# Block-sparse attention and Fourier mixing: clears ahead of the warm-up's copy, two q copies on ScalarE, fills in place of table operations, and a remade order

## Chip, cores, metric

One core of a Trainium2 chip. The metric is the device time of one execution in microseconds, here the median of three runs. A profile is one execution taken by the hardware profiler; its span runs from the first to the last instruction. Engines: TensorE (PE), VectorE (DVE), ScalarE (ACT), GpSimd (POOL), and SyncE (SP), which here only issues transfers.

## What is computed

Inputs q, k, v of shape (4, 8, 768, 64); each query block of 64 attends to its own key block and to the three blocks with the highest gate scores, causally. The result goes through a Fourier mixing layer and a two-layer perceptron with 512, 2048 and 512 features.

```python
k_rep = k.reshape(B, H, 12, 64, D).mean(axis=3)
gate = where(causal, einsum('bhsd,bhnd->bhsn', q, k_rep), -1e9)
sel = top 3 blocks of gate, and the own block
scores = where(sel & causal, scale * q @ k.T, -1e9)
x = softmax(scores) @ v                     # to (B, S, 512)
u = x + real(fft(fft(x, axis=1), axis=2))
un = (u - mean(u)) / sqrt(var(u) + 1e-6)
out = u + relu(un @ w_ch1) @ w_ch2
```

## The kernel before

Two heads make a pair P (0 to 15, four to a batch b). All work is cut into small steps with two-letter names, and the string `ORDER` (line 112) lists them; a loop at line 755 records them in that order. Each engine executes its own instructions in the order in which they stand in the list; between engines only semaphores order them. So a step can be listed late and still run early, if its engine's queue has nothing open ahead of it, and it can be held by a step that it has nothing to do with, if that one stands ahead of it on the same engine.

The steps of attention, with line and engine: loads `Lk`, `Lq`, `Lv` (L270, L275, SP queue); `tk`, `tq`, transposes of k and q on PE into PSUM (L292); `ks`, block sums of k on DVE (L297); `kh`, their spread to two heads (L222, DVE); `kc`, k to SBUF on ACT (L308, L311); `qc`, q to SBUF in f32 (L316, DVE); `qs`, q to f16 on POOL (L225); `g`, gate scores on PE (L335, L342); `gt`, their transpose and bounds on DVE (L349 to L358); `gx`, the eight largest of each row (L366); `gl:P,0`, the comparison with the third largest, and `gl:P,1`, the own block cleared (both L222, DVE); `gm`, transpose back, tile mt (L386); `s:P,i`, six score tiles (L409, L414), with mask products of mt and indz for P below 7 (L421); `e:P,i`, the exponential on ACT (L431); `d:P,i`, the triangle on POOL (L437); `vc`, v to f16 on POOL; `v`, attention times v on PE (L449); `x`, the division by the row sum on DVE.

The steps of mixing, for batch b: `fs`, `fd`, `f` folds on DVE; `pg`, a POOL instruction that waits for the folds, ahead of the weights' loads `W` and `X` (POOL queue); `y` on PE (L519, L525), `tr` on DVE (L538) and `ty` on ACT (L532); `m` on PE (L552, L553), `u` on DVE (L566), `xu` on ACT (L578), then the transposes: `xt` on PE and `un` on DVE in batch 0, DMA transposes on SP's queue (L593) in batches 1 to 3; `bn` statistics on DVE. The perceptron: `w` (L629, L631) and `r` (ReLU), then `c` in two halves (L656), `o` on DVE (L668) and `od`, the output's transfer.

PSUM is a pool of four tiles of two banks. If two engines read one such tile, the program makes the one that stands later in the list wait for the other: `ks` and `kc` of a pair, and `tr` and `ty` of one tile.

Before the list runs `consts_first` (L678 on): the first loads of k and q, half each on SP's and ACT's queues; a dummy exponential on ACT; nine warm-up matmuls on zeros, whose result DVE copies (L694); then on DVE a cast of the identity and six clears; and on ACT's queue the loads of three small tables: indc (block indicators, from which `iz:1` and `iz:0` make indz on ACT, L712), lim and oth. The table oth2 is loaded in `consts_next` on SP's queue.

Of the kernel before, what the change touches and what calls it, by code (L numbers as in the profile page):

```python
# [21 lines left out]
NB = 12  # L22
# [6 lines left out]
def _consts_np():  # L29
# [22 lines left out]
    oth = np.where(np.arange(9)[:, None] + 3 != nn, NEG, 0.0)[None].repeat(128, 0)  # L52

    lim = np.where(nn[None, 4:8] > np.arange(3, 7)[:, None], -3e38, 3e38)
    lim = lim.reshape(1, 16).repeat(128, 0).astype(np.float32)

    indc = np.zeros((4, 32, 2, NB), np.float32)
    for g in range(4):
        for n in range(NB):
            indc[g, n, g % 2, n] = 1.0  # L60

    own = 2 * np.arange(5)[None, :] + 2 + (p // 64)[:, None]
    oth2 = np.zeros((128, 5, 2, 16), np.float32)
# [49 lines left out]
Lk:1 Lq:1 Lk:2 Lq:2 tk:0 ks:0 tq:0 Lq:3 Lk:3 kh:0 qc:0 iz:1 tk:1 qs:0 kc:0 g:0 ks:1 iz:0 gt:0 tq:1  # L113
kc:1 gx:0 Lq:4 Lv:0 Lk:4 Lv:1 kh:1 gl:0,0 tk:2 gl:0,1 gm:0 kc:2 qc:1 s:0,3 s:0,2 ks:2 e:0,3 qs:1
tq:2 Lq:5 Lk:5 s:0,5 qc:2 g:1 e:0,5 e:0,2 kh:2 s:0,4 gt:1 qs:2 s:0,0 e:0,4 gx:1 s:0,1 d:0,2 tq:3
gl:1,0 e:0,0 gl:1,1 tk:3 gm:1 e:0,1 d:0,0 qc:3 g:2 d:0,3 kc:3 d:0,5 s:1,5 gt:2 d:0,4 s:1,0 e:1,5
qs:3 ks:3 s:1,4 e:1,0 tq:4 d:0,1 gx:2 vc:0 e:1,4 s:1,3 qc:4 s:1,1 Lv:2 e:1,3 s:1,2 gl:2,0 kh:3
tk:4 gl:2,1 e:1,2 d:1,3 gm:2 g:3 d:1,4 ks:4 d:1,0 v:0 d:1,5 gt:3 vc:1 kc:4 gx:3 e:1,1 s:2,5 Lv:3
Lq:6 LF:0 Lq:7 Lk:6 Lk:7 LT:0 s:2,3 kh:4 gl:3,0 e:2,5 gl:3,1 s:2,4 e:2,3 d:1,1 x:0 tq:5 qs:4 e:2,4
g:4 d:2,3 gm:3 qc:5 s:2,0 d:2,4 s:2,2 d:1,2 e:2,0 gt:4 d:2,5 tk:5 vc:2 gx:4 e:2,2 s:2,1 ks:5 d:2,0  # L120
Lv:4 Lq:8 Lk:8 s:3,1 e:2,1 v:1 gl:4,0 kh:5 gl:4,1 kc:5 d:2,1 gm:4 d:2,2 s:3,2 x:1 e:3,1 vc:3 g:5
e:3,2 Lv:5 Lc:0 d:3,1 s:3,5 gt:5 s:3,0 fs:0,1 e:3,5 s:3,3 d:3,2 gx:5 e:3,0 s:3,4 fs:1,1 tq:6
gl:5,0 e:3,3 fs:0,0 v:2 gl:5,1 fs:1,0 e:3,4 d:3,3 qc:6 d:3,0 s:4,5 x:2 d:3,4 s:4,4 e:4,5 d:3,5
s:4,0 qs:5 v:3 e:4,0 gm:5 fs:2,0 fs:2,1 e:4,4 s:5,5 x:3 s:4,1 e:5,5 s:5,1 e:4,1 fd:2,0 s:4,2 s:5,0
fs:3,1 e:5,1 fs:3,0 s:5,2 fd:2,1 e:5,0 fd:3,1 s:4,3 fd:3,0 e:5,2 tk:6 f:0,1 f:0,2 e:4,3 Lk:9 Lq:9
tk:7 f:0,3 e:4,2 f:0,0 y:0,1 ks:7 pg:0 W:0 kc:6 y:0,0 tr:0,1 d:4,0 kc:7 d:4,4 d:4,5 ks:6 d:5,5
d:4,1 ty:0,1 tr:0,0 s:5,3 d:5,2 s:5,4 d:4,3 kh:6 W:1 ty:0,0 m:0,2 qs:6 e:5,3 u:0,2 m:0,1 vc:4
e:5,4 m:0,0 u:0,1 xu:0,2 d:5,4 tk:8 d:5,1 d:4,2 u:0,0 xu:0,1 d:5,0 xt:0,2 W:2 g:6 un:0,2 xu:0,0
xt:0,1 gt:6 tq:8 un:0,1 kc:8 xt:0,0 qc:8 tq:7 un:0,0 qs:8 v:4 Lq:10 Lk:10 Lv:6 Lq:11 qc:7 bn:0,3
w:0,4 d:5,3 qs:7 bn:0,1 w:0,5 r:0,4 gx:6 ks:8 w:0,6 r:0,5 gl:6,0 kh:7 gl:6,1 x:4 w:0,7 r:0,6 gm:6  # L130
w:0,3 r:0,7 s:6,5 r:0,3 s:6,1 e:6,5 s:6,3 e:6,1 kh:8 s:6,2 fs:4,0 bn:0,4 w:0,2 e:6,2 d:6,1 X:0
e:6,3 g:7 w:0,0 d:6,5 gt:7 r:0,2 d:6,3 vc:6 gx:7 s:6,4 r:0,0 vc:5 s:6,0 e:6,4 tk:9 Li:0 gl:7,0
Lv:7 tq:9 gl:7,1 e:6,0 gm:7 w:0,11 Lq:12 Lv:8 K:7 qc:9 kc:9 g:8 r:0,11 v:5 gt:8 d:6,0 ks:9 w:0,8
qs:9 gx:8 w:0,10 x:5 r:0,8 d:6,4 d:6,2 gl:8,0 s:7,5 s:7,2 r:0,10 kh:9 fs:4,1 w:0,1 bn:0,5 e:7,5
vc:7 e:7,2 tq:10 gl:8,1 Lv:9 r:0,1 X:1 gm:8 s:7,4 qc:10 w:0,15 d:7,2 e:7,4 K:8 bn:0,0 g:9 r:0,15
s:7,0 w:0,9 gt:9 e:7,0 gx:9 vc:8 tq:11 r:0,9 d:7,0 Lv:10 s:7,1 qc:11 d:7,5 tk:10 d:7,4 e:7,1
gl:9,0 s:7,3 ks:10 v:6 e:7,3 kh:10 gl:9,1 kc:10 gm:9 d:7,3 s:8,4 bn:0,2 d:7,1 w:0,12 vc:9 x:6
e:8,4 K:9 Lv:11 Lk:11 Lq:13 Lq:14 Lk:12 Lk:13 v:7 r:0,12 g:10 x:7 s:8,3 w:0,13 e:8,3 gt:10 nv:0
s:9,4 r:0,13 fs:5,1 s:9,1 fs:7,0 vc:11 w:0,14 e:9,4 fs:6,1 e:9,1 fs:7,1 s:8,1 fs:6,0 fs:5,0
c:0,2,0 r:0,14 fd:7,1 fd:6,1 e:8,1 gx:10 s:9,0 fd:7,0 s:9,2 e:9,0 fd:6,0 s:8,2 gl:10,0 c:0,3,0  # L140
f:1,3 e:9,2 f:1,2 e:8,2 gl:10,1 f:1,0 s:8,0 gm:10 s:9,3 d:8,2 e:8,0 y:1,1 d:8,1 d:9,0 e:9,3 nr:0
c:0,0,0 tr:1,1 ty:1,1 s:9,5 c:0,2,1 e:9,5 d:8,0 d:9,3 tk:11 K:10 s:8,5 c:0,1,0 Lk:14 ks:11 kc:11
c:0,3,1 f:1,1 d:9,5 e:8,5 d:9,1 qs:10 tq:12 o:0,2 y:1,0 od:0,2 kh:11 d:8,4 o:0,3 pg:1 vc:10 qc:12
c:0,1,1 od:0,3 ty:1,0 d:9,4 Lv:12 Lv:13 qs:11 tr:1,0 g:11 c:0,0,1 gt:11 d:8,3 d:8,5 gx:11 qs:12
m:1,0 o:0,0 m:1,1 od:0,0 o:0,1 d:9,2 od:0,1 v:8 u:1,1 m:1,2 u:1,0 xu:1,1 c:0,4,0 gl:11,0 xu:1,0
un:1,1 x:8 s:10,3 gl:11,1 un:1,0 c:0,4,1 u:1,2 e:10,3 d:10,3 fs:8,0 s:10,5 s:10,2 bn:1,3 e:10,5
tk:12 e:10,2 fs:8,1 v:9 gm:11 Lk:15 Lq:15 ks:12 xu:1,2 K:11 bn:1,0 tq:13 kc:12 un:1,2 c:0,5,0
qc:13 vc:13 bn:1,4 s:11,2 d:10,5 x:9 s:11,4 vc:12 e:11,2 c:0,5,1 bn:1,1 Lv:14 Lv:15 e:11,4 s:11,0
o:0,5 s:11,5 w:1,11 e:11,5 od:0,5 o:0,4 e:11,0 kh:12 bn:1,5 od:0,4 s:11,3 w:1,7 e:11,3 r:1,11
s:10,1 d:11,3 r:1,7 d:11,0 s:10,0 e:10,1 d:11,4 g:12 d:10,2 tk:13 d:11,5 e:10,0 gt:12 d:11,2  # L150
s:11,1 ks:13 d:10,1 w:1,0 e:11,1 d:10,0 kh:13 fs:9,0 fs:9,1 s:10,4 r:1,0 d:11,1 gx:12 w:1,14
e:10,4 gl:12,0 gl:12,1 g:13 gm:12 r:1,14 d:10,4 w:1,12 K:12 gt:13 kc:13 gx:13 w:1,6 bn:1,2 r:1,12
tq:14 gl:13,0 r:1,6 qs:13 v:10 qc:14 gl:13,1 s:12,3 gm:13 s:12,5 v:11 x:10 e:12,3 K:13 e:12,5
s:12,0 x:11 w:1,8 e:12,0 fs:10,0 vc:15 s:12,1 r:1,8 s:12,2 fs:10,1 s:13,4 e:12,1 d:12,3 w:1,5
fs:11,1 d:12,5 e:13,4 fs:11,0 d:12,1 fd:10,0 w:1,10 r:1,5 fd:11,0 fd:10,1 s:13,0 fd:11,1 r:1,10
w:1,4 f:2,0 e:13,0 f:2,2 s:13,1 f:2,1 e:12,2 w:1,2 e:13,1 tk:14 r:1,4 w:1,3 ks:14 r:1,2 f:2,3
kc:14 s:12,4 kh:14 r:1,3 pg:2 y:2,0 d:13,4 vc:14 nv:1 e:12,4 qs:14 w:1,9 tr:2,0 w:1,13 ty:2,0
d:12,0 r:1,9 g:14 r:1,13 y:2,1 gt:14 gx:14 s:13,2 w:1,1 e:13,2 gl:14,0 gl:14,1 gm:14 s:13,5 w:1,15
tr:2,1 e:13,5 r:1,1 d:13,5 d:13,0 tk:15 ty:2,1 r:1,15 d:12,4 d:12,2 c:1,0,0 kc:15 nr:1 m:2,0 m:2,1
u:2,0 c:1,1,0 d:13,1 K:14 u:2,1 tq:15 ks:15 xu:2,1 s:13,3 bn:2,3 c:1,0,1 xu:2,0 un:2,1 qc:15  # L160
e:13,3 c:1,1,1 un:2,0 d:13,3 d:13,2 s:14,5 v:12 o:1,0 kh:15 od:1,0 o:1,1 v:13 e:14,5 bn:2,1 od:1,1
d:14,5 x:12 qs:15 s:14,3 m:2,2 e:14,3 bn:2,0 c:1,4,0 x:13 fs:13,0 g:15 fs:13,1 c:1,5,0 u:2,2
fs:12,0 xu:2,2 gt:15 c:1,2,0 bn:2,4 un:2,2 gx:15 c:1,5,1 gl:15,0 fs:12,1 gl:15,1 gm:15 bn:2,5
c:1,4,1 K:15 c:1,2,1 o:1,4 od:1,4 o:1,5 s:14,1 od:1,5 s:15,4 e:14,1 s:15,0 c:1,3,0 e:15,4 d:14,1
d:14,3 e:15,0 d:15,4 s:14,4 s:14,2 d:15,0 e:14,4 s:15,2 c:1,3,1 e:15,2 e:14,2 s:15,3 o:1,3 w:2,1
od:1,3 o:1,2 bn:2,2 w:2,2 od:1,2 r:2,1 s:15,5 w:2,4 e:15,5 w:2,15 r:2,4 r:2,2 w:2,3 r:2,15 e:15,3
s:15,1 r:2,3 d:15,3 w:2,9 d:14,4 e:15,1 d:14,2 d:15,2 d:15,5 s:14,0 r:2,9 d:15,1 w:2,14 e:14,0
v:15 d:14,0 w:2,5 x:15 w:2,7 r:2,5 fs:15,1 fs:15,0 r:2,14 fd:15,1 v:14 fd:15,0 r:2,7 w:2,6 x:14
w:2,11 fs:14,0 fs:14,1 fd:14,1 w:2,13 fd:14,0 f:3,2 f:3,0 w:2,10 r:2,13 r:2,11 w:2,8 f:3,3 r:2,10
f:3,1 nv:2 w:2,0 r:2,8 nr:2 r:2,6 y:3,1 r:2,0 y:3,0 ty:3,1 c:2,0,0 pg:3 tr:3,0 tr:3,1 w:2,12  # L170
c:2,1,0 r:2,12 ty:3,0 c:2,0,1 c:2,1,1 m:3,0 o:2,0 c:2,2,0 od:2,0 u:3,0 o:2,1 xu:3,0 m:3,1 od:2,1
c:2,4,0 u:3,1 un:3,0 xu:3,1 bn:3,2 m:3,2 c:2,3,0 u:3,2 un:3,1 bn:3,3 xu:3,2 c:2,5,0 bn:3,0 un:3,2
bn:3,5 c:2,3,1 bn:3,1 c:2,4,1 c:2,2,1 w:3,3 c:2,5,1 r:3,3 o:2,3 w:3,7 od:2,3 o:2,4 o:2,2 od:2,4
w:3,11 r:3,7 od:2,2 o:2,5 w:3,4 r:3,11 od:2,5 w:3,2 bn:3,4 nv:3 w:3,0 r:3,2 nr:3 w:3,8 r:3,0 w:3,1
r:3,8 w:3,13 r:3,1 r:3,4 w:3,6 w:3,10 w:3,9 r:3,10 r:3,13 w:3,5 r:3,6 w:3,14 r:3,5 w:3,12 c:3,2,0
r:3,12 r:3,9 r:3,14 c:3,0,0 w:3,15 c:3,4,0 r:3,15 c:3,1,0 c:3,0,1 c:3,1,1 c:3,5,0 o:3,0 od:3,0
o:3,1 c:3,3,0 od:3,1 o:3,5 od:3,5 c:3,4,1 c:3,2,1 o:3,4 od:3,4 c:3,3,1 c:3,5,1 o:3,3 od:3,3 o:3,2
# [610 lines left out]
```

## Time and profile before

| | |
|---|---|
| runs | 297.56, 297.54 and 297.93 us, median 297.56 |
| profiled execution, span | 295.6 us |
| PE busy | 286.5 us, 97% |
| DVE busy | 192.5 us, 65% |
| ACT busy | 164.2 us, 56% |
| POOL busy | 111.1 us, 38% |
| moved by DMA | 33.53 MB, mean 113 GB/s |
| granted TensorE clock | 1.00 |

Busy shares are means over stages with different limits. In a row of instruction groups stand the line, the engine, the operation, the tiles written and read with their shapes, the count, the busy us, the mean ns of one, and the idle time before it with what ended it. In a timeline row stand start, duration, engine (ACTq, SPq: the transfer queues of ACT and SP), line and operation. Two numbers joined by a dash or "from ... to" are start and end in the timeline, in us from the span's start.

### The profile page before, as it was taken

The numbers are of one execution on the slowest core, as the hardware profiler recorded it, in microseconds if no ns is written. First come the engines' busy times: TensorE is split into PE (matmuls) and PEld (weight loads), VectorE is DVE, ScalarE is ACT, GpSimd is POOL, SyncE is SP. The second block draws the span as 40 slices with busy tenths as digits, with TensorE's granted clock in tenths as the row PEclk, the third lists the DMA queues.
The fourth block names the chain that finished last, engine by engine and source line by source line (L and its number), as shares of the span: only waits on it lengthen the run. The fifth ranks groups of instructions, "written<-read, shape, count | busy, mean of one in ns | idle before, by whom it ended". The sixth has DMA issues, their size and how long they took to land.

```text
span 295.6 us, 6738 instructions
## 1 busy us (share of the span) xinstructions
PE 286.5 (97%) x2633; PEld 180.2 (61%) x2633; DVE 192.5 (65%) x597; ACT 164.2 (56%) x205; POOL 111.1 (38%) x286
## 2 busy tenths in 40 slices
PE   8899999999999999999999999999999999999995
PEld 4566767765676556656757667446666554555453
DVE  2999999986988638987796577714493282700132
ACT  3698989749578841677788843165524250155000
POOL 2267528528776289064753363220303000110000
PEclk9999999999999999999999999999999999999999
DMA  8999999997999727477000005311000052300023
GB/s 197 268 228 230 262 245 199 195 230 118 226 185 211 168 55 186 118 164 176 3 0 2 0 9 136 38 72 71 2 1 2 32 103 44 142 0 2 0 91 125
DMA packets 93200, 33.53 MB, mean 113 GB/s; under 512 B 85936, under 2 KB 89968, under 8 KB 93168
## 3 DMA queue, kind: packets, MB, share of 16 engines
q1 hardware_dynamic: 87504, 28.47, 40.6%
q0 software_dynamic: 3664, 4.19, 9.1%
q10 hardware_dynamic: 2000, 0.44, 0.7%
q8 instruction: 21, 0.34, 0.5%
q14 instruction: 11, 0.09, 0.1%
HBM read 28.63 MB, written 6.29 MB: 118 GB/s over the span
## 4 chain that ended last, share of the span: by engine, by line
PE 84%; DVE 7%; ACT 6%; DMA 1%; issue 1%; DVEq 0%; ACTq 0%
PE c L656 26%; PE h L629 19%; PE h L631 10%; PE sc L414 7%; PE av L449 6%; ACT pt L431 5%; PE tp L292 5%; PE yp L519 2%; PE mx L552 2%; DVE q L316 2%; PE mx L553 1%; PE warmps L693 1%; DVE u L566 1%; PE g L342 1%; PE c L648 1%; PE sc L409 1%
## 5 line engine op out<-in xcount | busy, mean ns | idle before, releaser
L431 ACT ACTIVATE pt<-sc 128x1024 f16<-128x1024 f32 (+1 forms) x96 | 83.3, 923 | 26.6 <-PE sc L414 19.7
L629 PE MATMUL h<-unT,w 128*128 128x512 f16 x256 | 85.1, 379 | 0.0
L656 PE MATMUL c<-w_sb,hT 128*128 128x512 f16 x368 | 83.8, 379 | 0.0
L631 PE MATMUL h<-unT,w 128*128 128x256 f16 x256 | 69.7, 272 | 0.4 <-DMA unT<-x 0.4
L641 ACT ACTIVATE hT<-h 128x768 f16<-128x768 f32 x48 | 37.8, 813 | 43.7 <-PE h L631 43.7
L656 PEld LDWEIGHTS <-hT 128*128 128x128 f16 x368 | 35.6, 98 | 39.3 <-issue 0.5
L437 POOL TENSOR_SCALAR_AFFINE_SELECT pt<-pt 128x256 f16<-128x256 f16 x96 | 37.5, 414 | 58.5 <-ACT pt L431 57.6
L629 PEld LDWEIGHTS <-w 128*128 128x128 f16 x256 | 25.0, 97 | 29.2 <-issue 1.3
L668 DVE SCALAR_TENSOR_TENSOR u<-c,rs,u 128x512 f32<-128x512 f32 (+1 forms) x25 | 17.5, 725 | 31.2 <-PE c L656 30.4
L639 DVE TENSOR_SCALAR hT<-h 128x768 f16<-128x768 f32 x16 | 15.3, 955 | 29.7 <-PE h L631 29.6
L578 ACT ACTIVATE x<-u,nm 128x512 f16<-128x512 f32 x24 | 15.9, 715 | 22.5 <-DVE nm L572 22.3
L292 PE MATMUL tp<-id,nat 128*128 128x128 f32 x192 | 27.5, 284 | 0.6 <-ACT pt L431 0.3
L631 PEld LDWEIGHTS <-w 128*128 128x128 f16 x256 | 25.0, 98 | 4.3
L225 POOL TENSOR_SCALAR_AFFINE_SELECT qk<-mt 32x160 f16<-32x160 f16 x72 | 23.1, 341 | 10.8 <-DVE mt L386 9.1
L414 PE MATMUL sc<-qk 96*128 96x512 f16 (+3 forms) x144 | 26.8, 305 | 0.0
L225 POOL TENSOR_SCALAR_AFFINE_SELECT qk<-q 64x768 f16<-64x768 f32 (+1 forms) x25 | 20.6, 825 | 14.8 <-DVE q L316 14.1
L292 PEld LDWEIGHTS tp<-id,nat 128*128 128x128 f32 x192 | 22.2, 146 | 5.7 <-issue 1.6
L449 PE MATMUL av<-v,pt 128*128 128x65 f16 x672 | 23.0, 193 | 0.1
L449 PEld LDWEIGHTS <-pt 128*128 128x128 f16 x672 | 22.0, 97 | 1.7 <-POOL pt L437 0.5
L297 DVE TENSOR_REDUCE kr<-tp 128x12 f32<-128x768 f32 x16 | 15.1, 945 | 5.9 <-PE tp L292 5.9
L222 POOL TENSOR_TENSOR t<-vr,rs 128x6 f32<-128x6 f32 x12 | 2.4, 199 | 43.5 <-DVE rs L609 42.9
L414 PEld LDWEIGHTS <-qk 96*128 96x128 f16 x144 | 13.3, 97 | 8.9 <-issue 0.5
(95 smaller groups left out, 351.2 us busy)
## 6 DMA issues: line engine op xcount, KB each, us to landing
nat<-in_v_dram SPq DMA_DIRECT2D x16, 384.0 KB, 4.7
nat<-in_k_dram SPq DMA_DIRECT2D x31, 192.0 KB, 3.5
nat<-in_q_dram SPq DMA_DIRECT2D x31, 192.0 KB, 3.9
out_dram<-u SPq DMA_DIRECT2D x23, 256.0 KB, 2.1
w_sb<-in_moe_w_ch_dram POOLq DMA_DIRECT2D x2, 1024.0 KB, 10.2
w<-in_moe_w_ch_dram POOLq DMA_DIRECT2D x2, 768.0 KB, 8.4
fs_sb<-c_FS SPq DMA_DIRECT2D x1, 582.0 KB, 5.1
w<-in_moe_w_ch_dram POOLq DMA_DIRECT2D x1, 512.0 KB, 7.3
```

The lines of the kernel that those rows point to most:

```text
L225: nc.gpsimd.affine_select(out=out, in_=in_, pattern=[[0, i] for i in n], base=0, channel_multiplier=0, compare_op=ALU.is_ge, fill=0.0)
L292: nc.tensor.transpose(ps[:, 128 * st:128 * st + 128], src[:, st, :], id32)
L414: nc.tensor.matmul(ps[:, e, co:co + q1 - q0], qk[0:96, e, 1, 128 * jt:128 * jt + 128], qk[0:96, e, 0, q0:q1], start=True, stop=True)
L431: nc.scalar.activation(out=d["pt"][:, o:o + 2 * n].rearrange("p (e c) -> p e c", e=2), in_=d["sc", i][:, :, 0:n], func=AF.Exp, scale=0.125)
L437: nc.gpsimd.affine_select(out=dg, in_=dg, pattern=[[0, 2], [1, 128]], base=0, channel_multiplier=-1, compare_op=ALU.is_ge, fill=0.0)
L449: nc.tensor.matmul(av[:, e, 66 * st:66 * st + 65], pt[:, co:co + 128], vv[:, e, jt, 0:65], start=(cnt == 0), stop=(cnt == 20))
L578: nc.scalar.activation(out=x_b[:, 2 * kp + k2, :], in_=u_b[:, k2, :], func=AF.Identity, scale=0.0625, bias=nm[:, k2:k2 + 1])
L629: nc.tensor.matmul(hp[:, 0:512], w1s, unT[:, dt, 0:512], start=(dt == 0), stop=(dt == NDT - 1))
L631: nc.tensor.matmul(hp[:, 512:768], w1s, unT[:, dt, 512:768], start=(dt == 0), stop=(dt == NDT - 1))
L641: nc.scalar.activation(out=hT, in_=hp, func=AF.Relu)
L656: nc.tensor.matmul(c_ps[b, g[0]][:, st - g[0], :], h_t[b, it][:, 128 * st:128 * (st + 1)], w2_sb[:, it, :], start=(it == 0), stop=(it == N ...
L668: nc.vector.scalar_tensor_tensor(out=o, in0=ps, scalar=st_t[b][1][:, st:st + 1], in1=o, op0=ALU.mult, op1=ALU.add)
```

## The change

It does five things. On DVE the six clears and the cast of the identity are issued ahead of the warm-up's copy; the copy itself is done by ACT, and its place in the program is ahead of the load of indc. The copies `qc:0` and `qc:1` are done by ACT. The bounds of the gates for P below 7, an elementwise minimum with the table lim, become a strided fill of the diagonal 4x4 blocks. The clearing of the own block, a product with the tables oth and oth2, becomes one strided fill (P below 7) or two (P from 7); for that the masks lt and ltb hold 0 and 1, and the factor -60000 moves into the indicators indc and ind. The loads of lim, oth and oth2 and the tables are gone. The list `ORDER` is written anew.

```diff
@@ a_q32
-        nc.vector.tensor_copy(out=q32, in_=pairs[P]["tp", 0])
+        if P < 2:
+            nc.scalar.copy(out=q32, in_=pairs[P]["tp", 0])
+        else:
+            nc.vector.tensor_copy(out=q32, in_=pairs[P]["tp", 0])
@@ g_turn, P < NX
-            x = gt.rearrange("p (b n) -> p b n", n=32)[:, 0:4, 4:8]
-            tt(x, x, lim, ALU.min)
+            nc.vector.memset(gt[:, 4:136].rearrange("p (b c) -> p b c", c=33)[:, :, 0:4], -3e38)
@@ g_less, j == 1
-            tt(l, l, o, ALU.mult)
+        elif P < NX:
+            nc.vector.memset(d["lt"][:, 3:268:33], 0.0)
+        else:
+            for w in range(2):
+                nc.vector.memset(ltb[64 * w:64 * w + 64, 2 + w:172 + w]
+                                 .rearrange("p (b c) -> p b c", c=34)[:, :, 0:17:16], 0.0)
@@ consts_first
-        nc.vector.tensor_copy(out=dummy, in_=wps[:, 0:1])
-        nc.vector.tensor_copy(out=id16, in_=id32)
         nc.vector.memset(half, 0.0)
...
         nc.vector.memset(ltb, 0.0)
+        nc.vector.tensor_copy(out=id16, in_=id32)
+        nc.scalar.copy(out=dummy, in_=wps[:, 0:1])
...
         nc.scalar.dma_start(indc, dr["indc"].ap())
-        nc.scalar.dma_start(lim, dr["lim"].ap().rearrange("p (b n) -> p b n", n=4))
-        nc.scalar.dma_start(oth, dr["oth"].ap().rearrange("p (b n) -> p b n", n=NB))
@@ consts_next
-        nc.sync.dma_start(oth2, dr["oth2"].ap().rearrange("p (b e n) -> p b e n", e=2, n=16))
@@ _consts_np
-            indc[g, n, g % 2, n] = 1.0
+            indc[g, n, g % 2, n] = NEG
-        ind[e, 16 * e:16 * e + NB] = nn[:, None] == (s[None, :] // 64)
+        ind[e, 16 * e:16 * e + NB] = NEG * (nn[:, None] == (s[None, :] // 64))
```

Of the list, the beginning, the first mixing and the last one:

```diff
-Lk:1 Lq:1 Lk:2 Lq:2 tk:0 ks:0 tq:0 Lq:3 Lk:3 kh:0 qc:0 iz:1 tk:1 qs:0 kc:0 g:0 ks:1 iz:0 gt:0 tq:1
-kc:1 gx:0 Lq:4 Lv:0 Lk:4 Lv:1 kh:1 gl:0,0 tk:2 gl:0,1 gm:0 kc:2 qc:1 s:0,3 s:0,2 ks:2 e:0,3 qs:1
...
-s:4,0 qs:5 v:3 e:4,0 gm:5 fs:2,0 fs:2,1 e:4,4 s:5,5 x:3 s:4,1 e:5,5 s:5,1 e:4,1 fd:2,0 s:4,2 s:5,0
-fs:3,1 e:5,1 fs:3,0 s:5,2 fd:2,1 e:5,0 fd:3,1 s:4,3 fd:3,0 e:5,2 tk:6 f:0,1 f:0,2 e:4,3 Lk:9 Lq:9
-tk:7 f:0,3 e:4,2 f:0,0 y:0,1 ks:7 pg:0 W:0 kc:6 y:0,0 tr:0,1 d:4,0 kc:7 d:4,4 d:4,5 ks:6 d:5,5
-d:4,1 ty:0,1 tr:0,0 s:5,3 d:5,2 s:5,4 d:4,3 kh:6 W:1 ty:0,0 m:0,2 qs:6 e:5,3 u:0,2 m:0,1 vc:4
-e:5,4 m:0,0 u:0,1 xu:0,2 d:5,4 tk:8 d:5,1 d:4,2 u:0,0 xu:0,1 d:5,0 xt:0,2 W:2 g:6 un:0,2 xu:0,0
-xt:0,1 gt:6 tq:8 un:0,1 kc:8 xt:0,0 qc:8 tq:7 un:0,0 qs:8 v:4 Lq:10 Lk:10 Lv:6 Lq:11 qc:7 bn:0,3
-w:0,4 d:5,3 qs:7 bn:0,1 w:0,5 r:0,4 gx:6 ks:8 w:0,6 r:0,5 gl:6,0 kh:7 gl:6,1 x:4 w:0,7 r:0,6 gm:6
...
-c:2,1,0 r:2,12 ty:3,0 c:2,0,1 c:2,1,1 m:3,0 o:2,0 c:2,2,0 od:2,0 u:3,0 o:2,1 xu:3,0 m:3,1 od:2,1
-c:2,4,0 u:3,1 un:3,0 xu:3,1 bn:3,2 m:3,2 c:2,3,0 u:3,2 un:3,1 bn:3,3 xu:3,2 c:2,5,0 bn:3,0 un:3,2
-bn:3,5 c:2,3,1 bn:3,1 c:2,4,1 c:2,2,1 w:3,3 c:2,5,1 r:3,3 o:2,3 w:3,7 od:2,3 o:2,4 o:2,2 od:2,4
...
+Lk:1 Lq:1 Lk:2 Lq:2 tk:0 tq:0 iz:1 tk:1 qc:0 ks:0 kh:0 Lq:3 qs:0 g:0 kc:0 kc:1 tq:1 ks:1 tk:2 iz:0
+gt:0 Lk:3 Lq:4 Lv:0 Lk:4 gx:0 gl:0,0 kh:1 gl:0,1 gm:0 s:0,3 s:0,5 qc:1 s:0,2 kc:2 e:0,5 tq:2 g:1
...
+e:3,3 x:2 s:4,4 s:4,0 fs:2,0 fs:2,1 d:3,0 d:3,1 d:3,4 d:3,3 qs:5 fd:2,0 v:3 s:5,5 e:4,5 e:4,4 e:4,0
+e:5,5 s:4,1 e:4,1 s:5,0 s:5,1 s:4,2 s:4,3 s:5,2 x:3 fs:3,1 fs:3,0 fd:2,1 fd:3,1 fd:3,0 f:0,2 f:0,3
+f:0,0 f:0,1 Lk:7 Lc:0 Lv:4 Lv:6 LT:0 LF:0 Lq:7 Lk:8 Lv:5 Lv:7 Lq:9 Lk:9 tk:7 e:5,1 y:0,1 e:4,2 y:0,0
+tr:0,1 s:5,4 e:4,3 e:5,2 ks:7 tk:6 tr:0,0 e:5,0 m:0,2 s:5,3 ks:6 kh:6 kc:7 ty:0,0 ty:0,1 m:0,1 u:0,2
+m:0,0 u:0,1 kc:6 tk:8 e:5,4 u:0,0 g:6 gt:6 e:5,3 d:4,1 vc:4 d:4,3 pg:0 W:1 d:4,4 d:4,5 d:5,1 d:5,2
+d:5,4 W:0 d:5,0 d:4,0 d:4,2 vc:6 W:2 vc:5 d:5,3 qs:6 d:5,5 xu:0,2 xu:0,1 xu:0,0 xt:0,2 xt:0,1 un:0,2
+un:0,1 tq:8 xt:0,0 un:0,0 gx:6 v:4 qc:8 w:0,4 r:0,4 w:0,5 r:0,5 kc:8 w:0,6 tq:7 w:0,7 bn:0,5 kh:7
...
+f:3,3 r:2,11 r:2,15 tr:3,0 r:2,9 c:2,1,1 ty:3,0 c:2,2,1 o:2,2 y:3,1 c:2,0,1 ty:3,1 m:3,0 c:2,4,0
+tr:3,1 o:2,1 o:2,0 u:3,0 m:3,1 u:3,1 c:2,4,1 m:3,2 bn:3,2 bn:3,3 c:2,5,0 c:2,3,0 c:2,3,1 c:2,5,1
+u:3,2 xu:3,0 xu:3,1 xu:3,2 od:1,4 od:1,2 od:1,3 od:2,1 od:2,0 od:2,2 un:3,0 un:3,1 un:3,2 o:2,4
+w:3,6 w:3,4 r:3,4 bn:3,0 bn:3,5 w:3,0 w:3,2 w:3,5 bn:3,1 r:3,2 w:3,13 o:2,5 bn:3,4 nv:3 r:3,5 nr:3
...
```

## The prediction

> **What bounds the kernel now.** I read the busy time by stretches of 10 us first, then the waits, then the timeline of the first 13 us, then the chain of work that ended last. In the first view the columns are the stretch, the sum, and the busy us (and instructions) of PE, PEld, DVE, ACT and POOL, then clock, DMA share and GB/s.
>
> ```profile
> 0.00:10.00 10.00, 8.13 (x39) 4.91 (x40) 4.54 (x15) 4.18 (x6) 2.50 (x18) 1.00 0.96 214
> 10.00:20.00 10.00, 9.10 (x114) 5.96 (x113) 9.48 (x37) 8.09 (x11) 4.63 (x10) 1.00 1.06 240
> 20.00:30.00 10.00, 9.56 (x160) 6.55 (x160) 9.73 (x46) 8.55 (x11) 7.00 (x15) 1.00 1.07 238
> 30.00:40.00 10.00, 9.68 (x228) 7.60 (x223) 8.85 (x32) 9.16 (x13) 5.00 (x11) 1.00 1.06 263
> 40.00:50.00 10.00, 8.83 (x114) 6.89 (x109) 9.85 (x21) 9.95 (x14) 4.54 (x11) 1.00 1.01 213
> 50.00:60.00 10.00, 9.39 (x119) 7.20 (x118) 9.67 (x25) 7.25 (x11) 6.31 (x11) 1.00 1.14 197
> 60.00:70.00 10.00, 10.00 (x95) 5.67 (x95) 7.92 (x39) 6.36 (x9) 3.90 (x7) 1.00 0.83 170
> ```
>
> Two regimes. From 10 to 58 us VectorE (DVE) and ScalarE (ACT) are both nearly full and TensorE (PE) waits for them. From 60 us to 292 PE is without a gap but for 0.4 us near 130. So a time saved or lost before the first `w:0,4` (timeline: 58.61) moves the end one to one; later, only new holes on PE count. Next, the first 13 us:
>
> ```profile
> 2.11 0.51 ACTq L707 DMA_DIRECT2D indc<-c_indc  x1
> ...
> 3.34 0.20 ACT L689 ACTIVATE dummy<-dummy 128x1 f32<-128x1 f32 x1
> 4.13 0.33 ACTq L709 DMA_DIRECT2D oth<-c_oth  x1
> ...
> 5.44 0.16 DVE L694 COPY dummy<-warmps 128x1 f32<-128x1 f32 x1 [4.19 <-PE warmps L693]
> ...
> 6.47 0.83 ACT L712 COPY indz<-indc 128x768 f16<-128x768 f16 x1 [2.92 <-DMA indc<-c_indc]
> 6.63 0.12 DVE L701 MEMSET ltb<- 128x80 uint32 x1
> 6.68 0.93 DVE L297 TENSOR_REDUCE kr<-tp 128x12 f32<-128x768 f32 x1
> ...
> 11.70 0.48 DVE L386 STREAM_TRANSPOSE mt<-lt 128x288 f16<-128x288 f16 x1
> ```
>
> The small table indc is asked for at 2.11 us and ACT's first useful work, `iz:1`, starts at 6.47 when it has landed. The selection chain ends with `gm:0` at 12.18, and the first exponential starts at 12.64.
>
> **The change, part by part, against the profiled span of 295.6 us** (the median of the runs is 297.56, so 1.96 lies around the span; I add it at the end).
>
> *Clears ahead of the copy: about nothing.* Six clears and the cast took DVE from 5.52 to 6.75. But `ks:0` waits for the first transposes of k, which end on PE at 6.62; it started at 6.68. At most 0.06 us is to be had.
>
> *The warm-up's copy on ACT: this is the price.* In the changed program the copy waits for two things, the nine warm-up matmuls and the dummy exponential, and, as on DVE today, the first wait is a semaphore instruction of its own ahead of the copy (DVE's records show one of L694 at 5.38 us, 21 ns). The load of indc is now the next thing on ACT's queue. Today oth, a load with a wait of its own, went out only at 4.13, a full 1.03 us after lim's was issued (2.65 + 0.45): a wait on this queue holds it. If the copy's does so too, indc is asked for at 5.45 instead of 2.11. The three small loads of this queue took 4.3, 4.1 and 3.4 us to land, mean 3.9: it lands at 8.85 to 9.75, I take 9.4, 2.9 us later than now. What stands behind it on ACT, in order: `iz:1`, `qc:0`, `kc:0`, `kc:1`. With 0.69 us from start to start (`kc:3` 18.09 to `e:1,5` 18.77) and 0.80 us for the last, `kc:1` ends at 9.44 + 2.07 + 0.80 = 12.3. On DVE `ks:1` now waits for `kc:1` and `gt:0` stands behind it: `ks:1` to 13.3 (0.95). `gt:0` to the end of `gm:0` took 2.52 (9.66 to 12.18), now 2.4: `gm:0` ends at 15.7. First mask products and scores, 0.65: first exponential at 16.4 instead of 12.64, +3.8 (bounds +3.2 to +4.1 from the landing alone).
>
> Row against rule: today indc's load went out at 2.11 although the ACTIVATE ahead of it ran only at 3.34, so work waiting on the engine does not hold the queue. [...] Whether a semaphore instruction on ACT holds a load behind it, no row of this case shows; that it does not is rival A.
>
> *q copies of pairs 0 and 1 on ACT.* DVE loses 0.95 + 0.92 us; ACT gains 2 x 0.80 (nearest row: the 128x768 cast of L308, 821 ns; upper end DVE's own 945). Both lie ahead of the first exponential, in time in which ACT waits anyway.
>
> *Fills for lim, oth and oth2.* Removed: the operations on lim, oth and oth2, in these rows, with the fill that is nearest.
>
> ```profile
> L222 DVE TENSOR_TENSOR ltb<-ltb,oth 128x120 f16<-128x120 f16 x9 | 3.3, 365 | 0.1
> L222 DVE TENSOR_TENSOR gt<-gt,lim 128x16 f32<-128x16 f32 x7 | 2.2, 309 | 0.2
> L222 DVE TENSOR_TENSOR lt<-lt,oth 128x108 f16<-128x108 f16 x7 | 1.5, 215 | 0.1
> L356 DVE MEMSET gt<- 64x10 f32 x9 | 0.6, 67 | 0.6
> ```
>
> A strided fill is bounded by 62 ns (smallest fill) and the operation that it replaces; I take 65 to 67. DVE saves 7 x 0.244 + 7 x 0.15 + 9 x 0.23 = 4.8 us, of which 6 pairs, 2.4 us, before `w:0,4`. After 60 us DVE has 2 us and more free in most stretches, and PE's own work hides the rest. Three loads fall away (lim and oth on ACT's queue, oth2 on SP's).
>
> *What the remade order recovers.* From the first exponential to the last of pairs 0 to 3, 12.64 to 36.99, ACT worked 22.27 and waited 2.08. Part of the waits was for DVE (`kc:4` waited 0.82 for `ks:4`), which is now lighter by 4.3 us. I let ACT wait 1.0 (between 0 and 2.08): last exponential of these pairs at 16.4 + 22.3 + 1.0 = 39.7, +2.7. From there to the end of `tr:0,0` it was 2.52 to `x:3` and 9.5 more; `ks:6` (0.95) now stands behind it and `fd:2,0` (0.55) ahead of `x:3`: 39.7 + 2.5 + 8.0 = 50.2. Both `ty` copies now stand behind `tr:0,0`, and `kc:6`, `e:5,4`, `e:5,3` between them and the three `xu`. By start-to-start times: 50.25 + 2 x 0.95 + 0.7 + 2 x 0.9 + 4.13 (the `xu` took 51.76 to 55.89) = 58.8, +2.9. `xt:0,0` and `v:4` on PE (0.6 + 1.44): `w:0,4` at 60.85, +2.2. `tq:7` (0.65 by PE's spacing) stood ahead of it and now follows: +2.9 at the end.
>
> *Later holes on PE.* In the last batch the chain from `m:3,2` through `u`, `xu` and the transposing transfers sets `w:3,*`:
>
> ```profile
> 237.74 8.38 SPq L593 DMA_TRANSPOSE unT<-x  x6
> ```
>
> `m:3,2` ended at 240.05, the last of these six started at 244.9 and landed 2.5 later, 7.35 in all; PE had 8.65 of work between. The new order leaves four half rows of c there, 4 x 1.73 = 6.9, and puts two `bn` (1.75) ahead of `u:3,2` on DVE, which costs another 0.55: a hole of 0.8 or so. In batch 1 PE's work between `m:1,2` and `w:1,11` grows by 0.8, so of the hole of 0.85 around 132 us half may close: -0.4. Sum of both +0.4, bounds -0.8 and +2.
>
> *Moved and covered.* The weights (`W:1`, 768 KB, 8.4 us) go out on POOL's queue behind `d:4,3` and the end of f:0, near 47 to 48, so land near 56, ahead of `w:0,4`; if not, `w:0,4` waits one for one. fs_sb stands on SP behind `Lv:6`, which waits for `vc:3`: asked for near 40, 5.1 us to land, `y:0,1` needs it near 46.5; this cover is 1 us or so.
>
> **Sum:** 2.9 + 0.4 = +3.3, span 298.9, with 1.96 around it 300.9 us.
>
> **Rivals.**
> - A, the other side: the wait does not hold the queue, indc lands at 6.4. Then `qc:0` starts at 7.64 behind `tq:0`, `gm:0` ends near 13.3, the first exponential starts at 13.95 (+1.3), and the lighter DVE lets ACT lose all its waits to 55.89 (2.98 us): `xu:0,0` ends 1.7 earlier, `w:0,4` 2.3 earlier, end -2.3 + 0.65 = -1.65: 295.9. For it: the row at 2.11 and the full DVE. Against it: the separate semaphore instruction. It decides if indc is asked for before 3 us; with ACT keeping half its waits it shrinks to no change.
> - B, the delay is mostly absorbed: indc late, but ACT runs without a wait from 16.4 on: `xu:0,0` at 16.4 + 40.3 = 56.7, `w:0,4` +0.1, end +0.75 and up to +0.4 for holes: 298.5. Against it: `ty:0,0` waits for `tr:0,0`.
> - C, nothing is recovered: +3.8 and `tq:7` reach the end, and the tighter order opens holes of 2 us: +6.4, 304.0.
>
> **How the numbers follow.** The sum above 0.64, A 0.13, B 0.14, C 0.09. I give the sum's case 299.5 to 302.5. To leave out no more than 2 in 10 the range takes in B and the lower part of C, from 298.0 to 303.6. A measurement of this kernel can tell about 0.2% (0.6 us) from no change. Faster: most of A, 0.11. Same: the rest of A and the edge of B, 0.05. Slower: 0.84.
>
> **What would show it.** indc's load on ACT's queue at 5.4 to 5.5 us and `iz:1` at 9 to 10; first exponential at 16 to 17; `w:0,4` at 60 to 61.5; a hole of about 1 us on PE just ahead of the first h of batch 3. I am wrong if indc goes out at 2 us, if `w:0,4` starts before 58.6, or if PE shows holes of more than 2 us in all after 62 us.

## The result, and the profile after

The changed kernel took 315.55 us (median of 4 runs, 314.66 to 316.11) against 297.61 us: a ratio of 1.060, 95% interval 1.058 to 1.062. It is slower by 18 us where 3.3 was forecast, and outside the forecast's range of 298.0 to 303.6. The profiled execution spans 312.5 us, 16.9 more than before; PE is busy 289.0 us and idle 23.5, where it was idle 9.1 before.

First the busy time by stretches of the changed kernel (columns as in the forecast: stretch, sum, PE, PEld, DVE, ACT, POOL, then clock, DMA share, GB/s):

```profile
0.00:10.00 10.00, 6.85 (x27) 3.78 (x27) 2.51 (x11) 2.32 (x4) 1.66 (x17) 1.00 1.04 180
10.00:20.00 10.00, 6.98 (x68) 4.05 (x70) 5.61 (x23) 6.72 (x11) 2.15 (x4) 0.83 1.36 219
...
50.00:60.00 10.00, 7.90 (x85) 5.96 (x83) 7.94 (x21) 7.58 (x10) 4.81 (x12) 1.00 0.82 147
60.00:70.00 10.00, 8.58 (x102) 6.28 (x102) 6.47 (x22) 6.17 (x9) 3.95 (x6) 1.00 1.18 211
110.00:120.00 10.00, 8.99 (x71) 5.95 (x70) 2.99 (x7) 7.08 (x8) 8.62 (x28) 1.00 0.01 2
200.00:210.00 10.00, 8.04 (x74) 4.18 (x73) 4.11 (x23) 3.35 (x4) 3.46 (x11) 1.00 0.40 105
```

Three things are new. The first 20 us hold 13.8 us of PE work instead of 17.2. The DMA engines are busier there (1.36 against 1.06) and yet move less (219 GB/s against 240). And behind 60 us, where PE had no gap but one, it now has many. `w:0,4` starts at 64.16 instead of 58.61 (+5.6); from there to the end of DVE's last instruction it is 244.8 us instead of 234.1 (+10.8). The output's last transfer ends 3.6 us after that instead of 2.9.

Then the start, in the timeline:

```profile
5.45 0.35 ACTq L697 DMA_DIRECT2D indc<-c_indc  x1
...
8.29 0.85 PE L276 MATMUL tp<-id,nat 128*128 128x128 f32 x6 [0.84 <-DMA nat<-in_k_dram]
9.32 0.83 ACT L700 COPY indz<-indc 128x768 f16<-128x768 f16 x1 [3.73 <-DMA indc<-c_indc]
10.06 0.79 ACT L301 COPY q<-tp 128x768 f32<-128x768 f32 x1
10.75 1.50 ACT L292 CAST qk<-tp 128x768 f16<-128x768 f32 x2
...
12.29 0.96 DVE L281 TENSOR_REDUCE kr<-tp 128x12 f32<-128x768 f32 x1 [4.57 <-ACT qk L292]
...
15.03 0.48 DVE L376 STREAM_TRANSPOSE mt<-lt 128x288 f16<-128x288 f16 x1
...
16.07 1.44 ACT L421 ACTIVATE pt<-sc 128x256 f16<-128x256 f32 x2 [1.69 <-PE sc L411]
```

This is the forecast's chain, each link within 0.4 us: indc asked for at 5.45, `iz:1` at 9.32 (forecast 9.4), `ks:1` held by `kc:1`, `gm:0` done at 15.51 (15.7), first exponential at 16.07 (16.4). The chain is right; what each link of it costs is another question, and the runs below answer it differently. One line is not in the forecast: `tk:1` at 8.29 waited 0.84 us for the load of k.

PE's waits over the whole span, longest sums first (the semaphore's source, us, times, longest):

```profile
PE sc L411 <- DVE mt L376: 2.3, 2, 1.9
PE h L619 <- ACT hT L631: 2.2, 2, 1.3
PE tp L276 <- ACT qk L295: 1.8, 1, 1.8
PE g L322 <- ACT q L301: 1.8, 1, 1.8
...
PE sc L404 <- POOL qk L212: 1.3, 1, 1.3
...
PE c L646 <- ACT qk L295: 1.0, 1, 1.0
```

Most stand for one or two waits each: single places, behind different steps of DVE, ACT and POOL, not one slow resource. Waits for transfers are a small part of it: 0.8 us for k at the start, 0.4 for unT. One of the places, in the timeline of the later part:

```profile
201.76 0.75 DVE L658 SCALAR_TENSOR_TENSOR u<-c,rs,u 128x512 f32<-128x512 f32 x1 [2.74 <-PE c L646]
202.43 0.34 DVE L340 STREAM_TRANSPOSE gt<-g 128x160 f32<-128x160 f32 x1
...
204.87 2.67 POOL L212 TENSOR_SCALAR_AFFINE_SELECT qk<-mt 32x160 f16<-32x160 f16 x8 [4.71 <-DVE mt L376]
...
207.30 0.51 PE L404 MATMUL sc<-qk 96*128 96x128 f16 x2 [1.25 <-POOL qk L212]
...
208.43 0.75 PE L439 MATMUL av<-v,pt 128*128 128x65 f16 x19 [0.62 <-POOL pt L427]
```

Read it backwards. `s:15,5` waits 1.25 us for POOL's `K:15`, which idled 4.71 for the gates of pair 15, whose first DVE step `gt:15` ran at 202.43 directly behind `o:1,5`. DVE had stood idle for 2.74 us, waiting to do `o:1,5`, and for most of that time `gt:15` stood ready behind it: its input `g:15` ended on PE at 199.89. If so, the order of DVE's list alone made the hole; moving `gt:15` ahead is tried below.

The fills cost 66 to 72 ns where 65 to 67 was forecast (groups: count, busy us, mean ns, idle before):

```profile
L370 DVE MEMSET ltb<- 64x10 f16 x18 | 1.2, 67 | 1.1
...
L337 DVE MEMSET gt<- 128x16 f32 x7 | 0.5, 72 | 0.3
L367 DVE MEMSET lt<- 128x9 f16 x7 | 0.5, 66 | 0.1
```

### The profile page after: what moved, and what is told of

Read it like the earlier page. It is cut to its first block, busy times and chain, and to the rows that moved or that the text cites. A ratio compares the mean times of both kernels' runs of the same rounds, so it can differ in the third digit from the quotient of the medians.

```text
span 312.5 us, 6737 instructions
## 1 busy us (share of the span) xinstructions
PE 289.0 (92%) x2633; PEld 180.3 (58%) x2633; DVE 191.2 (61%) x603; ACT 165.9 (53%) x208; POOL 112.7 (36%) x286
## 4 chain that ended last, share of the span: by engine, by line
PE 71%; DVE 15%; ACT 7%; DMA 2%; issue 2%; POOL 1%; SPq 0%; ACTq 0%; DVEq 0%; POOLq 0%
PE c L646 21%; PE h L619 16%; PE h L621 8%; PE sc L404 6%; PE av L439 5%; PE tp L276 5%; DVE kr L281 2%; ACT qk L295 2%; DVE u L556 2%; ACT ty L522 2%; PE mx L542 1%; PE yp L509 1%; PE warmps L683 1%; PE sc L399 1%; PE mx L543 1%
## 5 line engine op out<-in xcount | busy, mean ns | idle before, releaser
L658 DVE SCALAR_TENSOR_TENSOR u<-c,rs,u 128x512 f32<-128x512 f32 (+1 forms) x25 | 17.6, 719 | 28.3 <-PE c L646 27.3
L212 POOL TENSOR_SCALAR_AFFINE_SELECT qk<-mt 32x160 f16<-32x160 f16 x72 | 23.2, 343 | 19.3 <-DVE mt L376 17.6
```

What stands on the lines that cost most here:

```text
L212: nc.gpsimd.affine_select(out=out, in_=in_, pattern=[[0, i] for i in n], base=0, channel_multiplier=0, compare_op=ALU.is_ge, fill=0.0)
L658: nc.vector.scalar_tensor_tensor(out=o, in0=ps, scalar=st_t[b][1][:, st:st + 1], in1=o, op0=ALU.mult, op1=ALU.add)
```

## The experiments

Three theories at first. H: the held load of indc is the main cost. L: the remade list opens holes. E: the edits themselves cost.

**One part at a time.** *The load ahead of the copy in the changed kernel:*

```diff
+        nc.scalar.dma_start(indc, dr["indc"].ap())
         nc.scalar.copy(out=dummy, in_=wps[:, 0:1])
```

> The changed kernel, with the load of indc issued ahead of the warm-up's copy again. Theory H (the held load is the main cost): iz:1 back at 6.4, first exponential near 14, w:0,4 near 59, time 303 or less. Rival L (the remade list itself leaves chains without slack, whatever the start): the start comes back by 2 to 3 us, the holes on PE after w:0,4 stay at 10 us, time 310 to 313.

314.82 us, ratio 1.055 (1.050 to 1.060). `iz:1` starts at 7.65 instead of 9.32 and the first exponential at 14.40 instead of 16.07, but `w:0,4` only at 63.20 instead of 64.16. H falls as the main cost, and the time is above L's 310 to 313 as well. What the load is worth this run does not settle: in its trace the chain to `w:0,4` comes from `vc:3`, which waits for a load of v that lands at 38.80, so that a later load hides part of the gain.

*All edits, with the list of before:*

> All edits of the change, but the list of before; the load of indc still stands behind the copy. H: near 301, the load still held. L: 296 to 299, since the old list has qc:0 ahead of iz:1 and gt:0 not behind kc:1. Rival E (the edits themselves cost: the q copies on ScalarE or the strided fills): 305 or more.

300.35 us, ratio 1.006 (1.004 to 1.009), between H and L.

*Before, with the remade list and nothing else:*

> The kernel before, with the remade list alone: copies of q on VectorE, tables lim and oth, load of indc at 2.1. H: 297 to 300. L: 308 to 313. E: near 298.

317.42 us, ratio 1.064 (1.060 to 1.067). L alone makes the whole loss, and more than the 308 to 313 expected; the first exponential starts at 14.68 with indc asked for as early as ever.

*Before, with the warm-up's copy on ACT ahead of the load:*

```diff
-        nc.vector.tensor_copy(out=dummy, in_=wps[:, 0:1])
+        nc.scalar.copy(out=dummy, in_=wps[:, 0:1])
```

> The kernel before, with one line changed: the warm-up's copy on ScalarE, ahead of the load of indc. H: the load goes out at 5.4, lands near 9.3, and 2 to 4 us reach the end: 299.5 to 301.5. L: the old list has nothing but iz:1 and the casts of k behind it, within 1 us of before: 297.6 to 298.6.

297.48 us, ratio 0.998 (0.997 to 0.999). indc is asked for at 5.45 and `iz:1` starts at 8.23 instead of 6.47, and no cost reaches the end: in the old list `ks:1` stands ahead of `kc:1`, so the selection chain does not pass through ACT, and the first exponential starts at 12.37 (12.64 before).

**Where in the list.** *The remade list up to `w:0,4`, the old order behind it, with the edits:*

> The changed kernel's edits; its list up to the first h product (w:0,4), and from there on the order of before. If the list's cost lies where its holes are seen (start +5.6 us to w:0,4, and 10 to 11 us of PE holes behind it), 303 to 304 us. If the holes behind w:0,4 are only the late start's echo (buffers and operands late all through), they stay with this start and it takes 312 to 316. If the start's loss is absorbed by slack of the old order behind it, 298 to 301.

305.03 us, ratio 1.026 (1.023 to 1.029), a little over the 303 to 304 of the first case. `w:0,4` starts at 66.18, and from there to the end it is 234.1 us, as before: the later holes are no echo of the late start, but belong to the order in which they stand.

*The other half:*

> The other half: the changed kernel's edits, the order of before up to w:0,4 and the remade order behind it. If the holes belong to the remade order where they stand, 310 to 312 us (300.4 of the old list with all edits, and 10 to 11 of holes), with the same holes at w:0,7 (1.4), c:0,0,0 (1.05), s:15,5 (1.4) and w:3,0 (1.1). If they were the late start's echo, 300 to 302 and no such holes.

313.74 us, ratio 1.056 (1.051 to 1.061). `w:0,4` at 60.62 and the holes at `w:0,9`, `c:0,0,0`, `s:15,5` and `w:3,0` at their old places and lengths (0.75, 1.05, 1.42, 1.12 from start to start). But the hole at `w:0,7` is missing, and the splice made one of its own: `s:7,2` waited 4.5 us. So this run shows where holes sit, and its total is not a price.

**The edits on the old list.** *The q copies alone, on before:*

> Before, with the first two q copies on ScalarE and nothing else. If these copies are what makes the edits on the old list cost 0.6% (they stand in ScalarE's start between iz:1 and kc:0, which the old list had laid for a lighter ScalarE), 299 to 300.5 us and a first exponential 1 us or more later; if the fills, the clears or the held load do it, 297.0 to 298.0.

297.48 us, ratio 0.999 (0.998 to 1.001). Nothing.

*All edits but the q copies, old list:*

> All edits but the q copies, on the old list. If the q copies on ScalarE are the cost of the edits, 295 to 297.5 us: each gate then does one cheap fill in place of a min or a product, and two loads are gone; if the clears or the fills are the cost, 299.5 to 301, as with the q copies.

300.45 us, ratio 1.010 (1.008 to 1.013). So the fills, the clears or something that comes with them cost 3 us. The traces showed a fourth candidate, A: in every kernel that drops the tables, the 256-byte packets of the first 20 us took 24.1 to 24.4 ns on the mean (packet records of the traces); in every kernel that keeps them, 18.0. The tables lim, oth and oth2 (216, 64 and 320 bytes a partition) lay in SBUF, the on-chip memory, ahead of the tiles nat into which q, k and v are loaded. Without them, and with ltb 64 bytes larger, all later tiles moved down by 544 bytes a partition in the program's layout (the sizes alone sum to 536). By that layout the tiles of q and k began on a multiple of 256 before; 544 bytes lower is 224 past one.

*Before, with an unused tile ahead of the large ones:*

```diff
     half = ctile([128, 2, NB], FP, "half")
+    ctile([128, 112], F16, "pad")
```

> Before, with an unused tile of 224 bytes a partition ahead of the large tiles and nothing else: the input tiles nat then begin 224 bytes past a multiple of 256, as they do in the changed kernel, where before has them on one. New theory A (address): dropping lim, oth and oth2 moved these tiles, and a 256-byte packet to such an address takes about 24 ns instead of 18, which is what the edits cost on the old list. By A, 299.5 to 301 us and a q1 share of the DMA of about 43% of the span; by its rival (the fills or the clears cost it), 297.0 to 298.0.

299.67 us, ratio 1.0065 (1.0048 to 1.0082). An edit that changes nothing but addresses costs 2 us. The load queue's line before (packets, MB, share of 16 engines):

```profile
q1 hardware_dynamic: 87504, 28.47, 40.6%
```

and with the shifted tiles, for the same packets:

```profile
q1 hardware_dynamic: 87504, 28.47, 44.9%
```

and what PE does about it, in the timeline of the same run; these three waits for loads are not there before. All other tiles behind the unused one moved too, but the engines' operations took the same time: 946 ns against 945 for the block sums of k on DVE, 800 in both for the casts of k on ACT, 827 against 825 for q on POOL.

```profile
8.54 0.85 PE L293 MATMUL tp<-id,nat 128*128 128x128 f32 x6 [1.06 <-DMA nat<-in_k_dram]
...
10.49 0.85 PE L293 MATMUL tp<-id,nat 128*128 128x128 f32 x6 [0.48 <-DMA nat<-in_q_dram]
12.29 0.85 PE L293 MATMUL tp<-id,nat 128*128 128x128 f32 x6 [0.96 <-DMA nat<-in_k_dram]
```

*The edits without the q copies, old list, with 32 bytes that put the tiles back on a multiple of 256:*

> The edits without the q copies, on the old list (300.4 us as measured), plus an unused tile of 32 bytes that puts the nat tiles back on a multiple of 256 bytes. By A 295.5 to 297.5 us, so that the fills bring 0 to 2 us once the address is repaired; if the fills or the clears cost, 300 to 301 as without the 32 bytes.

297.22 us, ratio 0.998 (0.997 to 1.000). *With the q copies too:*

> All edits, the q copies on ScalarE with them, on the old list and with the 32 bytes (300.35 us without them). By A 296 to 298 us; if the edits themselves cost, 300 to 301.

297.68 us, ratio 1.000 (0.998 to 1.001). E falls: on the old list the address was the cost of the edits, within the noise of these runs (0.2%). *The changed kernel with the 32 bytes:*

> The changed kernel with the same 32 bytes and nothing else. If address and list add up, 311.5 to 313.5 us (315.6 less some 3), the remade list still costing 14 or more; if the remade list's holes are only what slow loads make of it, 297 to 303; if the address is nothing, 315 to 316. First exponential ahead of 15 us by A, 16.1 without it.

314.42 us, ratio 1.057 (1.053 to 1.061). Packets of 18.0 ns again, and the first exponential at 14.51; the list's cost stays. The time lies between two of the cases: address and list do not simply add up.

*Before, shifted by 64 bytes:*

> Before, with an unused tile of 64 bytes, so that the nat tiles of q and k begin 64 bytes past a multiple of 256 and still on one of 64. If a 256-byte packet is slow wherever it starts off a multiple of 256, packets of 24 ns in the first 20 us and 299.5 to 300.5 us, as with 224 bytes; if 64 is what counts, packets of 18 ns and 297.0 to 298.2 us.

300.18 us, ratio 1.008 (1.005 to 1.010), packets of 24.7 ns. A multiple of 64 is not enough.

**Single places or the whole list?** From the changed kernel with the 32 bytes (314.42 us), a few steps are moved within the list. The trace of that kernel is its slowest run, 317.08 us, with three drops of the clock (last section); so the medians below are the safer measure, and the times inside the traces show places rather than prices. *Two in the start:*

```diff
-tk:1 qc:0 ks:0 kh:0 Lq:3 qs:0 g:0 kc:0 kc:1 tq:1 ks:1 tk:2
+tk:1 qc:0 ks:0 kh:0 ks:1 Lq:3 qs:0 g:0 kc:0 kc:1 tq:1 tk:2
-tr:0,1 s:5,4 e:4,3 e:5,2 ks:7 tk:6
+ks:7 tr:0,1 s:5,4 e:4,3 e:5,2 tk:6
```

> The changed kernel with the 32 bytes (314.4 us), and two positions of the list changed: ks:1 goes back ahead of kc:1 (the two read one PSUM tile and run one after the other, so that gt:0 stood behind kc:1), and ks:7 ahead of tr:0,1 (kc:7 and so tk:6 waited for it). If single positions make the holes: gm:0 ends 12.5 instead of 13.95 us, the hole at tk:6 is 1.0 instead of 1.8, and the time 311.5 to 313. If the loss is spread, 314 to 315, the holes reappearing further on.

310.23 us, ratio 1.043 (1.040 to 1.046). `gm:0` ends at 12.61 and `w:0,4` starts at 59.23 instead of 64.69.

*Six behind `w:0,4`, two of them shown here:*

```diff
-w:0,4 r:0,4 w:0,5 r:0,5 kc:8 w:0,6 tq:7 w:0,7 bn:0,5 kh:7 ks:8
+kc:8 ks:8 w:0,4 r:0,4 w:0,5 r:0,5 w:0,6 tq:7 w:0,7 bn:0,5 kh:7
-s:14,0 o:1,5 c:1,3,0 s:14,2 gt:15 xu:2,0 gx:15 gl:15,0 gl:15,1 gm:15
+s:14,0 gt:15 gx:15 gl:15,0 gl:15,1 gm:15 o:1,5 c:1,3,0 s:14,2 xu:2,0
```

> The changed kernel with the 32 bytes, and six positions behind w:0,4 changed: kc:8 and ks:8 ahead of w:0,4; r:0,3 ahead of gl:7,1; gt:10 ahead of fs:6,0; kc:11 ahead of ty:1,1; gt:15 to gm:15 ahead of o:1,5; o:2,5 and o:2,3 ahead of bn:3,0. Their holes are 1.26 (w:0,7), 0.43 (w:0,11), 0.64 (w:0,9), 0.99 (c:0,0,0), 1.27 and 0.62 (s:15,5 and v:13), 0.96 (w:3,0): 6.2 us. If single positions make the holes, 308 to 310 us; if the loss is spread, 312.5 to 315.

305.73 us, ratio 1.026 (1.023 to 1.028). From `w:0,4` to the end of DVE's last instruction it is 237.4 us instead of 246.7, and `s:15,5` no longer waits. *Both sets:*

> Both sets of moves. If holes of single positions add up, 306 to 308 us; if the later part takes up what the start gives, as the two other runs will show, 308 to 311; if spread, 312.5 to 315.

302.54 us, ratio 1.016 (1.013 to 1.019): moves at eight places in a list of 1011 steps take back 12 of the list's 17 us, more than expected, as each set alone did. PE's longest waits of this kernel:

```profile
PE g L323 <- ACT q L302: 1.5, 1, 1.5
...
PE yp L510 <- DVE fg L492: 1.2, 1, 1.2
...
PE tp L277 <- ACT qk L296: 0.8, 1, 0.8
PE sc L412 <- DVE mt L377: 0.7, 1, 0.7
```

The lines for hT and POOL's qk have left the top. The first is `g:0` waiting for `qc:0`, which stands behind `iz:1`. So *the load ahead of the copy once more:*

> The changed kernel with the 32 bytes, both sets of moves (302.5 us) and the indc load issued ahead of the warm-up's copy. In the run with all moves iz:1 still starts at 8.0 us, qc:0 behind it ends 9.5 and g:0 waits 1.46 for it. If the held load was masked by the list, iz:1 now starts at 6.5 and g:0 at 8.3, and the time is 301.0 to 301.8; if ScalarE's queue has another limit, iz:1 or g:0 stay and it takes 302.3 to 302.8.

301.31 us, ratio 1.012 (1.010 to 1.014). `iz:1` starts at 6.50, `g:0` at 8.08 instead of 9.59. Here the held load is worth 1.2 us by the medians, though the two intervals just overlap. Of the 3.7 us that are left, smaller places of the same kind are 2.0 (0.4 at `v:11`, 0.7 at `c:1,4,0`, 0.9 at `w:3,6`, start to start), and `tq:7`, which stands behind `w:0,4`, would be 0.65 by the forecast; the rest stays open.

*Fills and clears on the old list, without the costs found:*

> The old list with the fills and the clears, q copies on VectorE, the 32 bytes, and the indc load ahead of the copy: what the experiments leave of the change once each cost is taken out. The same with the load held took 297.2 us at a ratio of 0.998. If the held load still costs there, 296.0 to 296.8; if not, 297.0 to 297.5.

296.77 us, ratio 0.996 (0.995 to 0.998): faster than the kernel before, by about 1 us (297.59 in the same series). Against the same with the load held (0.998, 0.997 to 1.000) the intervals overlap; what the load adds there is not settled.

## Why the prediction was wrong

*Direction and first chain: right, in part by luck.* Behind the semaphore instruction ahead of the copy (5.37 on ACT in the trace) the load went out at 5.45, as the sum's case had it; which of the two held it, that instruction or the copy (5.43), no run tells apart. The times to the first exponential came within 0.4 us. But 9.4 for `iz:1` was right for a reason that the forecast did not have: held in the same way, with the tiles of q and k where they were before, `iz:1` started at 8.23; the rest, up to 9.32, goes with the slow packets.

*The price of the held load: wrong.* The forecast put +3.8 us at the first exponential down to it. Moving the load alone gives back 1.7 of it, the 32 bytes alone 1.6, and the list has +2.0 with neither. The links lie over one another: `iz:1` at 9.32 is hold and slow packets together, and `gm:0` follows ACT only because the remade list has `ks:1` behind `kc:1`. On the old list no cost of the hold reached the end.

*What the remade order recovers: the first step that failed.* Forecast 39.7 for the last exponential of pairs 0 to 3; it ended at 40.91, ACT having waited 2.7 us on the way where 1.0, and at most 2.08, was allowed. Most of that miss is the drop of the clock at 16.35 (last section): in two other traces with the same list there, without a drop in this stretch, ACT waited 1.5 us (load ahead) and 1.3 (new list, then old, where that exponential ended at 39.90). From there `w:0,4` was set by adding up spacings along ACT: 60.85, and it was 64.16. That sum knew `ty` behind `tr:0,0`, but had no `kc:7`:

```profile
51.35 0.94 DVE L281 TENSOR_REDUCE kr<-tp 128x12 f32<-128x768 f32 x1
...
52.38 1.60 ACT L295 CAST qk<-tp 64x768 f16<-64x768 f32 x2 [2.77 <-DVE kr L281]
...
54.03 0.87 PE L276 MATMUL tp<-id,nat 128*128 128x128 f32 x6 [1.77 <-ACT qk L295]
```

`ks:7` (51.35) stands behind the folds and `tr:0,1` on DVE, `kc:7` waits 2.8 us for it, and `tk:6` 1.8 us for the PSUM tile that `kc:7` frees. A tile held by a step late in another engine's order was not priced.

*Later holes on PE: the step that cost most.* +0.4 was forecast, with a bound of +2, from looking at two places of 230 us (batch 3 and the hole of batch 1). One was found as forecast: `w:3,6`, 0.5 against 0.8 (the forecast's own terms, 7.35 + 0.55 - 6.9, give 1.0). But there were 9.3 us of holes at thirteen other places (time from start to start above what the form usually takes: `w:0,7` 1.4, `c:0,0,0` 1.1, `s:15,5` 1.4, `w:3,0` 1.1 and smaller); at those whose chain was followed, a PSUM tile or an operand had its releaser put behind other work. The forecast's ground, that PE's own work hides what happens after 60 us, was a property of the old list; it was carried over to a list that was not read there. Rival C named the mechanism, at 2 us and a chance of 0.09, and the forecast's own sign of being wrong, more than 2 us of holes after 62 us, came true.

*Clears, q copies, fills: right as to their own time.* With the tiles on a multiple of 256, all edits together on the old list took 297.68 us, no change, and the q copies alone 297.48; the fills took 66 to 72 ns. But "three loads fall away" was priced as a gain only. What the dropped tables moved in SBUF was not asked, and that is 2 to 3 us on the old list.

Not told apart: how much of the changed kernel's own 18 us is the address. There the 32 bytes gave 1.1 us, with intervals that overlap, and the two traces differ in the clock as well.

## What to carry to other kernels

When an order is written anew, read all of it against the old one: for each PE step, which step frees its tile or writes its operand, and what now stands ahead of that on its engine; a stretch without gaps proves nothing about another order. Test an edit and a new order apart, for the order can cost more than all edits together. After tiles are removed or resized, look at where the tiles that DMA fills now begin (a shift by 224 bytes cost 2 us here).

## What the runs showed of the hardware

*Address and packets.* 256-byte packets, the pieces in which q, k and v are loaded, took 18.0 ns (mean of the first 20 us) where q's and k's tiles begin on a multiple of 256 bytes, and 24.1 to 24.7 ns where they begin 64 or 224 past one; the rate from 3 to 15 us was 272 GB/s before and 219 with the tiles shifted. Two things limit this. Not all such packets of the changed kernel are slow: they took 24.0 to 25.7 ns from 4 to 22 us (mean of each 2 us), but 17.8 to 21.3 from 22 to 42; and those of the loads of q and k at 122.52 and 123.68, the first loads since 102.23, took 17.6 to 18.0 (mean of each us). And for v, whose tiles by the layout begin 128 past a multiple in the kernel of before, no rule comes out. In that kernel 74,773 of 82,944 such packets took 18 ns, which leaves at most 8,171 others for v's 24,576. But of the 3,072 packets of its two loads of v at 112.75 the last sixth took 25.0 ns, where the last sixth of as many for k and q, from 125.89 on, took 18.2.

*The clock.* In the changed kernel the clock granted to PE fell to one half for 3.41 us. Three stretches of its windows (columns as above):

```profile
12.90:16.35 3.45, 1.33 (x26) 0.73 (x24) 3.27 (x17) 1.76 (x4) 0.00 (x0) 1.00 1.35 218
16.35:19.77 3.42, 3.42 (x23) 1.77 (x22) 1.52 (x4) 2.04 (x3) 1.09 (x2) 0.50 1.38 222
19.77:23.20 3.43, 3.43 (x54) 2.43 (x49) 2.96 (x15) 3.22 (x4) 0.93 (x2) 1.00 1.15 200
```

PE had worked 1.33 of the 3.45 us ahead; for the next 3.42 the granted clock is 0.50, then 1.00 again. The six transposes of one step took 1.54 us there and 0.85 at 8.29. Kernels on the old list showed no such dip before their last matmul. Those with the remade list, or a half of it, showed none to three, at 10.6 to 16.4, 53 to 55, 78 or 209 to 211 us, each of 3.41 us and one of twice that. Ahead of each, some stretch of 3.4 us held 1.8 us or more of PE idle time; but not every such stretch led to one (the changed kernel idled 1.96 of the 3.4 us from 51.7 on, without). Right ahead of each dip PE had been busy for 0.8 to 1.8 of 3.41 us; what brings a dip on, no run shows. At a granted clock of 0.50 a dip of 3.41 us costs at most half its length, 1.7 us by estimate, and less where PE waits anyway; so if holes bring the dips, a hole can cost more than its length, which was not tried by itself. A dip is the smaller part of what the later moves gave back beyond their holes (9.3 us in the traces, for waits of 6.2): counted from start to start, as above, the holes that went are about 8 us, and a dip at 209.70, in the trace without the moves alone, about 1.
